# A third early expert slot, the last weight sums outside the fixed order, and a later fetch of the late slots' tables

## The chip, the cores and the metric

The kernel runs on one core of one Trainium2 chip. The metric is the device time of one execution in microseconds (us). Before the change the median of 3 runs is 879.53 us (878.68 to 882.45).

## The reference: what is computed

Two stages follow each other. The first is a hashed attention: 4 batches, 8 heads, 768 positions, 64 values a head. Each query and each key gets a bucket from the signs of six projections, a query looks only at keys of its own bucket, and the softmax of the masked scores weighs the values.

```python
mask = q_bucket[:, :, :, None] == k_bucket[:, :, None, :]
scores = scale * np.matmul(q, k.transpose(0, 1, 3, 2))
scores = np.where(mask, scores, -1000000000.0)
...
x = np.ascontiguousarray(attn_out.transpose(0, 2, 1, 3)).reshape(B * S, H * D)
```

The second is a mixture of experts over the 3072 tokens x of 512 values: each token goes to the one expert of eight with the largest logit and is weighted by its softmax.

```python
logits = x @ w_gate + modality_bias[modality_id]
e_idx = np.argmax(logits, axis=1)
...
    h = np.maximum(x[mask] @ w1[e], 0.0)
    out[mask] = gate_w[mask, None] * (h @ w2[e])
```

With the inputs as drawn two experts get nearly all tokens: after the first three batches (2304 tokens) experts 1 and 3 have 1124 and 1099 of them, which is four full blocks of 256 tokens each, eight in all.

## The kernel before, in words

**Attention stage.** Heads are taken in pairs, 16 pairs, four to a batch. The PE's order in this stage is written out by hand (`tc.manual_schedule` over PE in `attention`, with the string `PLAN`): scores, exponentials, row maxima and the weighing of the values of neighbouring pairs are interleaved. For each pair `score` lets POOL (sometimes DVE) add up the exponentials over the key tiles (line 326), and `sums` (line 359) multiplies the result with ones on PE, so that the weights' sums stand ready for the division. In the order of PE `sums(i - 1)` stands inside of the next pair (letter Q); that of the last pair, `sums(NPR - 1)` at line 514, stands at the end of the fixed order.

**After a batch.** `finish(b)` (lines 366 to 412) projects the batch's result on the gate weights, turns it and divides it, and its last part, `route` (lines 589 to 636), finds each token's expert and place and writes the tokens' records into the table `tab` in DRAM with six indirect DMAs of POOL (line 631, the scatter). `finish_x` (lines 415 to 427) turns the attention result itself, divides it and writes it to `x_d` in DRAM, six tiles a batch, through two buffers `xs` (DVE line 424, DMA line 426; for the last batch on ACT's queue). For the first three batches these steps lie inside of the fixed order of a later batch.

**Expert stage.** The work is cut into slots. A big slot has 256 tokens of one expert, a small one 128. A slot runs through eight pieces of weights: pieces 0 to 3 are quarters of `w1` (`gemm1`, lines 793 to 795), pieces 4 to 7 quarters of `w2` (`gemm2`, lines 835 to 837). `Runner.slot(k)` (line 882 and on) runs them. `ahead` keeps SP loading weights (lines 748 and 750, 512 KB a piece) up to seven pieces ahead in four buffers, and ACT and DVE (for odd pieces of the first eight POOL) splitting them in a high and a low part (lines 756 and 758). `fetch` reads a slot's expert and place from the slot table, reads its token records with a DMA of SP (line 766, `tb`) and gathers the tokens' rows from `x_d` with one indirect DMA of POOL for each 128 tokens (line 770, `xg`). `prepare` also turns the rows on PE (line 781, eight transposes for a big slot) and splits them (ACT line 782, DVE line 783). In slot k the next slot is prepared at piece 4; the two slots after it are fetched at piece `CFG["fj"]`, which is 0, when k > 0.

**Early and late slots.** The first `EARLY` = 2 slots ("e") hold only full blocks of tokens of the first three batches, so that their tables are known before the last batch is through. `early_slots` finds them. Then `body` fetches and prepares slot e0, fetches e1, and because EARLY is 2 runs all of `finish(3)`, then `late_slots` (some forty small DVE operations, lines 642 to 713), and only then slot 0, interleaved with `finish_x(3)`. The late slots are 12 - EARLY = 10 big ones ("b") and 2 small ones ("s"). Their records come from `tab`, so that SP's read of it waits for the scatter, and their rows from `x_d`, so that POOL's gather waits for all writes of it. The gather of an early slot reads only the rows of the first three batches; its read of `tab` waits for those scatters that stand ahead of it in the program. More than the sure number of slots run in conditional blocks behind the last slot; with these inputs none does, 12 big and 2 small slots cover all tokens.

**Order.** Outside of the fixed order an instruction's place on its engine is found when the program is built, by its place in the program and by when its inputs are expected. Each engine then works through its list in order; whatever waits holds all behind it.

Of the kernel before, what the change touches and what calls it, by code (L numbers as in the profile page):

```python
# [18 lines left out]
B, H, S, D = 4, 8, 768, 64  # L19
# [3 lines left out]
REST = S - MAIN  # L23
NP = B * H // 2
BIG = 2.0 ** 100
CFG = dict(spd=(15,), fxs=3, wy=(0.3, 0.71), hpf=0, he=0, hn=0, hm=0, avp=(1, 2, 3, 4, 5, 6), avs=(2,), early=2, w3=(0, 0.9), x3=(0, 1), nmd=1, man=(), man0=2, hpo=0, hpe=0, p0=(0, 1), p1=(0, 0.25), p2=(0, 0.4), p3=(0.4, 0.9), s0=4, rc='DDDD', rq=(1, 2), tq=(3, 3, 1, 1, 0, 0), wh=(0.5, 0.78), ws=(0.78, 1.05), n2=2, psx=2, psm=2, pss=2, npb=4, ut=8, qk=3, v=2, wm=(0, 0.9), wf=(0.04, 1.02), wx=(0.3, 0.71), sub="DPPD", fx='D', fx3='R', raw=4, wp=7, LS=4, LL=7, pn=8, rv=(0,), rs='DDPP', r1=(0, 0.5), r2=(0, 1), avg=1, fub=2, fd=2, pm=(), fj=0, fxe=1.0)
P = 128

LAG = 2
# [45 lines left out]
def attention(ctx, actx, tc, a, x_d, l_d, route=None, setup=None):  # L75
    nc = tc.nc
    q, k, v, proj = a["q"], a["k"], a["v"], a["proj"]
    NPR = a.get("npair", NP)
    fconst = ctx.enter_context(tc.tile_pool(name="fconst", bufs=1))
    spool = ctx.enter_context(tc.tile_pool(name="spool", bufs=2))  # L80
    upool = ctx.enter_context(tc.tile_pool(name="upool", bufs=CFG["ut"]))
    bp = ctx.enter_context(tc.tile_pool(name="bp", bufs=1))
    ps_x = ctx.enter_context(tc.tile_pool(name="ps_x", bufs=CFG["psx"], space=PSUM))
    nat = actx.enter_context(tc.tile_pool(name="nat", bufs=CFG["n2"]))
    ld = actx.enter_context(tc.tile_pool(name="ld", bufs=CFG["qk"]))
    gens = []
    for g in range(3):
        opp = actx.enter_context(tc.tile_pool(name=f"opp{g}", bufs=1))
        gens.append({n: [opp.tile([P, S], F32R, name=f"{n}_{h}g{g}") for h in range(2)] for n in ("m1", "s1", "m2", "s2")})
    ldv = actx.enter_context(tc.tile_pool(name="ldv", bufs=CFG["v"]))  # L90
    sm = actx.enter_context(tc.tile_pool(name="sm", bufs=4))
    const = actx.enter_context(tc.tile_pool(name="const", bufs=1))
    ps_m = actx.enter_context(tc.tile_pool(name="ps_m", bufs=CFG["psm"], space=PSUM))
    ps_s = actx.enter_context(tc.tile_pool(name="ps_s", bufs=CFG["pss"], space=PSUM))
# [5 lines left out]
    def load(i, heads=(0, 1)):  # L100
        b, c = i // 4, i % 4
        t = st.setdefault(i, {"qk": []})
        for h in heads:
            qk = ld.tile([P, 2, NT, D], F32, name="qk")
            t["qk"].append(qk)
            for x, src in enumerate((q, k)):
                nc.sync.dma_start(out=qk[:, x], in_=src[b, 2 * c + h].rearrange("(p t) d -> p t d", t=NT))

    def load_v(i):
        b, c = i // 4, i % 4  # L110
        t = st[i]
        t["v"] = ldv.tile([P, 2, NT, D], F32, name="vt")
        nc.sync.dma_start(out=t["v"], in_=v[b, 2 * c:2 * c + 2].rearrange("h (p t) d -> p h t d", t=NT))
# [238 lines left out]
    def sums(i):  # L352

        b, c = i // 4, i % 4
        if c == 0:
            gsum[b] = bp.tile([P, HALF], F32, name="gs")
        g = ps_x.tile([P, MAIN], F32, name="psx")
        for j in range(4):
            nc.tensor.matmul(g[32 * j:32 * j + 32, 0:HALF], ones[:, c], st[i]["sp"][:, j // 2, (j % 2) * HALF:(j % 2 + 1) * HALF],
                             start=True, stop=True, tile_position=(0, 32 * j))  # L360
        if c == 0:
            nc.vector.tensor_copy(out=gsum[b], in_=g[:, 0:HALF])
        else:
            nc.vector.tensor_tensor(out=gsum[b], in0=gsum[b], in1=g[:, 0:HALF], op=ALU.add)
# [80 lines left out]
    with tc.manual_schedule(engines={mybir.EngineType.PE}):  # L445
        load(1)
        load_v(0)
        load(2)
        first()
        wg = sm.tile([P, 4, 8], F32, name="wg", bufs=1)  # L450
        nc.sync.dma_start(out=wg, in_=a["moe_w_gate"].rearrange("(c p) e -> p c e", p=P))
        gst = fconst.tile([P, 4, 32], F32, name="gst")
        nc.gpsimd.memset(gst, 0.0)
        nc.gpsimd.tensor_copy(out=gst[0:64, :, 0:8], in_=wg[0:64])
        nc.gpsimd.tensor_copy(out=gst[64:128, :, 16:24], in_=wg[64:128])
        ones = fconst.tile([P, 4, 32], F32, name="ones")
        nc.gpsimd.memset(ones, 0.0)
        for c in range(4):
            nc.gpsimd.memset(ones[:, c, c:c + 1], 1.0)
        if setup is not None:  # L460
            setup()
        avs = weigh()
        fins = xs = ts = iter(())
        for i in range(NPR):
            late = []
            ss = score(i)
            ms = maxp(i + 1, late) if i + 1 < NPR else iter(())
            last, ts = ts, chain(turn(i + 2), signs(i + 2), patterns(i + 2)) if i + 2 < NPR else iter(())
            ws = split(i + 3) if i + 3 < NPR else iter(())
            if i % 4 == 0 and i > 0:  # L470
                fins = finish(i // 4 - 1)
            for kt in range(NT):
                for c in PLAN[kt]:
                    if c == "S":
                        next(ss)
                    elif c == "M":
                        next(ms, None)
                    elif c == "T":
                        next(ts, None)
                    elif c == "P":  # L480
                        next(last, None)
                    elif c == "W":
                        next(ws, None)
                    elif c == "A":
                        if i > 0 or kt >= LAG:
                            next(avs)
                    elif c == "B":
                        if late:
                            late.pop(0)()
                    elif c == "v":  # L490
                        vadds(i)
                    elif c == "V":
                        vsums(i)
                    elif c == "Q":
                        if i > 0:
                            sums(i - 1)
                    elif c == "L":
                        if i + 3 < NPR:
                            load(i + 3)
                    elif c == "l":  # L500
                        if i + 1 < NPR:
                            load_v(i + 1)
                    elif c == "F" and i % 4 == 0 or c == "f" and i % 4 == 1:
                        next(fins, None)
                    elif c == "e" and i % 4 >= 2 or c == "E" and i == NPR - 2:
                        next(fins, None)
                    elif c == "x" and i % 4 == 2 or c == "y" and i % 4 == 3:
                        if c == "x" and kt == 0 and i > 4:
                            xs = finish_x(i // 4 - 1, 0, NT)
                        next(xs, None)  # L510
                        next(xs, None)
        for _ in avs:
            pass
        sums(NPR - 1)
    return finish, finish_x, ps_x, ident


# [6 lines left out]
EARLY = CFG["early"]  # L524
# [194 lines left out]
def experts(ctx, tc, a, x_d, tab, out, ps_x, ident):  # L719
# [3 lines left out]
    raw = ctx.enter_context(tc.tile_pool(name="raw", bufs=CFG["raw"]))  # L723
# [122 lines left out]
    class Runner:  # L846
# [35 lines left out]
        def slot(self, k):  # L882
            s = self.order[k]
            nxt = self.order[k + 1] if k + 1 < len(self.order) else None
            self.prepare(s)
            hh, hl, h = [], [], None
            for j in range(8):
                self.ahead()
                if j == CFG["fj"] and k > 0:
                    for s2 in self.order[k + 1:k + 1 + CFG["fd"]]:  # L890
                        self.fetch(s2)
                if j == 4:
                    yps = [ps_y.tile([P, DM], F32, name="yps") for _ in range(nt(s))]
                    if nxt:
                        self.prepare(nxt)
                hi, lo = self.ws.pop(self.n)
                if j >= 4:
                    gemm2(j, hi, lo, hh, hl, yps)
                elif nt(s) == 2:
                    gemm1(hi, lo, *self.xs[s], hh, hl)  # L900
                else:
                    last, h = h, gemm1_small(hi, lo, *self.xs[s])
                    if last is not None:
                        turn_small(last, hh, hl)
                if j == 4 and h is not None:
                    turn_small(h, hh, hl)
                self.n += 1
                yield
            store(self.got[s][0], yps)
# [73 lines left out]
```

## Time and profile before

| what | us |
|---|---|
| median of 3 runs | 879.53 |
| lowest, highest | 878.68, 882.45 |
| profiled execution, its own time | 876.6 |
| its span, first to last instruction | 874.7 |
| PE busy | 815.4 (93%) |
| DVE busy | 584.8 (67%) |
| ACT busy | 506.2 (58%) |
| POOL busy | 457.1 (52%) |

The profile was taken from one execution. The span is what the rows' times count from; 876.6 - 874.7 = 1.9 us lie outside of it. PE is the tensor engine, DVE the vector engine, ACT the scalar engine, POOL GpSimd, SP the engine that issues most DMAs. A busy PE is not a PE at its peak: matmuls overlap, and the time from one start to the next (0.12 us for a 256-column one in the expert stage) is shorter than what a row gives as one's duration.

### The profile page before, as it was taken

The page shows a single profiled execution, that of the slowest core. Times are in us where ns is not written, and L with a number is a line of the kernel's source. Part 1 is how long each engine was busy: PE and PEld are TensorE (multiplying, and loading weights), DVE is VectorE, ACT ScalarE, POOL GpSimd, SP SyncE. Part 2 cuts the span into 40 slices and gives each one's busy share as a digit, 9 for nine tenths or more (in the row PEclk, how much of TensorE's full clock was granted, in tenths as well). Part 3 has the DMA queues.
Part 4 walks back from the last instruction along what each step waited for, and adds up shares of the span by engine and source line. Part 5 has one row for each costly group of instructions (what it writes and reads, how often), then busy time and mean ns, then how long its engine had stood idle before and what let it go on. Part 6 is the DMA issues. An engine that isn't in the chain of part 4 may idle for free.

```text
span 874.7 us, 14543 instructions
## 1 busy us (share of the span) xinstructions
PE 815.4 (93%) x5154; PEld 579.8 (66%) x5154; DVE 584.8 (67%) x1029; ACT 506.2 (58%) x953; POOL 457.1 (52%) x347
## 2 busy tenths in 40 slices
PE   5899999998999998999998898879999999999993
PEld 3555655654665554665554555779999999998993
DVE  7776676678677678667776876955555555667550
ACT  5666766665666565566664364444555555557551
POOL 5387678757688757687756687322222221123010
PEclk9899999999999999999999999999999999999997
DMA  6423212221332321340210163796777776677750
GB/s 178 115 60 91 64 41 77 74 54 55 98 85 72 91 60 32 97 118 22 55 46 9 31 229 120 166 266 196 230 231 218 222 227 215 209 240 267 229 155 22
DMA packets 76753, 110.87 MB, mean 127 GB/s; under 512 B 10495, under 2 KB 52095, under 8 KB 76672
## 3 DMA queue, kind: packets, MB, share of 16 engines
q1 hardware_dynamic: 70880, 95.14, 37.6%
q0 software_dynamic: 4928, 13.14, 4.0%
q10 hardware_dynamic: 864, 1.57, 0.9%
q8 instruction: 43, 0.70, 0.4%
q14 instruction: 38, 0.31, 0.1%
HBM read 84.83 MB, written 13.33 MB: 112 GB/s over the span
## 4 chain that ended last, share of the span: by engine, by line
PE 77%; DVE 10%; ACT 4%; DMA 3%; issue 3%; POOL 2%; SPq 0%; POOLq 0%; ACTq 0%; DVEq 0%
PE psu L341 14%; PE pss L305 8%; PE pss L306 6%; PE psm L239 5%; PE yps L835 5%; PE yps L837 5%; PE yps L836 5%; PE hps L795 4%; PE hps L794 4%; PE hps L793 4%; PE psx L207 3%; PE psx L180 3%; PE psm L245 3%; PE psx L222 2%; DVE mx L241 1%
## 5 line engine op out<-in xcount | busy, mean ns | idle before, releaser
L326 POOL TENSOR_TENSOR sp<-sp,pb 128x768 f32<-128x768 f32 x124 | 225.3, 1841 | 42.0 <-ACT pb L323 40.6
L758 DVE TENSOR_TENSOR w<-raw,w 128x1024 fp32r<-128x1024 f32 x108 | 134.9, 1250 | 94.4 <-ACT w L756 93.3
L756 ACT CAST w<-raw 128x1024 fp32r<-128x1024 f32 x112 | 117.2, 1047 | 63.2 <-PE yps L837 55.9
L341 PE MATMUL psu<-pb,vt 128*64 128x512 f32 (+1 forms) x768 | 147.0, 505 | 0.0
L241 DVE TENSOR_REDUCE mx<-psm 128x1 f32<-128x512 f32 x192 | 127.6, 685 | 23.1 <-PE psm L239 22.4
L318 ACT ACTIVATE pb<-pss 128x512 f32<-128x512 f32 x192 | 114.9, 599 | 42.3 <-PE pss L306 22.8
L323 ACT ACTIVATE pb<-pss 128x512 f32<-128x512 f32 x96 | 57.5, 599 | 125.7 <-PE pss L306 122.8
L793 PE MATMUL hps<-xh,w 128*128 128x256 f32 x384 | 108.9, 284 | 2.4 <-DVE hl L800 2.4
L794 PE MATMUL hps<-xl,w 128*128 128x256 f32 x384 | 108.9, 284 | 0.0
L795 PE MATMUL hps<-xh,w 128*128 128x256 f32 x384 | 108.5, 283 | 0.0
L341 PEld LDWEIGHTS psu<-pb,vt 128*64 128x64 f32 x768 | 47.2, 137 | 88.4 <-issue 88.2
L770 POOL DMA_INDIRECT xg<-x_d,tb x26 | 30.8, 1184 | 125.9 <-DMA tb<-tab 87.7
L843 POOL DMA_INDIRECT out<-y,tb x26 | 34.0, 1309 | 118.0 <-ACT y L842 61.3
L835 PE MATMUL yps<-w,hl 128*128 128x512 f32 x208 | 83.6, 402 | 1.9 <-DVE hl L823 1.9
L837 PE MATMUL yps<-w,hh 128*128 128x512 f32 x208 | 81.8, 393 | 0.0
L836 PE MATMUL yps<-w,hh 128*128 128x512 f32 x208 | 81.7, 393 | 0.0
L247 DVE TENSOR_REDUCE mx<-psm 128x2 f32<-128x512 f32 x96 | 66.1, 689 | 22.7 <-PE psm L245 21.5
L305 PE MATMUL pss<-m_0g,s_0g 128*128 128x512 f32 x192 | 78.2, 407 | 0.0
L793 PEld LDWEIGHTS hps<-xh,w 128*128 128x128 f32 x384 | 73.4, 192 | 3.7 <-DVE hl L800 3.0
L166 POOL TENSOR_TENSOR n<-qk,n 128x384 fp32r<-128x384 f32 x36 | 39.7, 1109 | 67.3 <-ACT n L162 60.0
L794 PEld LDWEIGHTS hps<-xl,w 128*128 128x128 f32 x384 | 73.6, 192 | 1.7 <-issue 1.2
L795 PEld LDWEIGHTS hps<-xh,w 128*128 128x128 f32 x384 | 73.5, 192 | 0.0
(214 smaller groups left out, 1763.0 us busy)
## 6 DMA issues: line engine op xcount, KB each, us to landing
raw<-moe_w SPq DMA_DIRECT2D x112, 512.0 KB
qk<-q SPq DMA_DIRECT2D x32, 192.0 KB
qk<-k SPq DMA_DIRECT2D x32, 192.0 KB
vt<-v SPq DMA_DIRECT2D x16, 384.0 KB
x_d<-xs SPq DMA_DIRECT2D x18, 256.0 KB
m_1g<-m_1g SPq DMA_DIRECT2D x16, 192.0 KB
s_1g<-s_1g SPq DMA_DIRECT2D x16, 192.0 KB
m_0g<-m_0g SPq DMA_DIRECT2D x15, 192.0 KB
```

Of the source, the lines that this page charges most:

```text
L241: nc.vector.tensor_reduce(out=mx[:, qt + j, hi, 0:1], in_=mp, axis=AX.X, op=ALU.max)
L305: nc.tensor.matmul(out, t["s1"][h][:, ks], t["m1"][h][:, cs], start=True, stop=False)
L326: (nc.vector if h and i in CFG["spd"] else nc.gpsimd).tensor_tensor(out=t["sp"][:, h], in0=(t["pb"][0] if kt == 1 else t["sp"])[:, h], in1 ...
L341: nc.tensor.matmul(t["u"][part][64 * h:64 * h + 64, 0:w], t["v"][:, h, kt], t["pb"][kt][:, h, COLS[part]], start=False, stop=(kt == NT - 1 ...
L756: nc.scalar.copy(out=hi, in_=r)
L758: (nc.gpsimd if pool else nc.vector).tensor_tensor(out=lo, in0=r, in1=hi.bitcast(F32), op=ALU.subtract)
L793: nc.tensor.matmul(hps, lo[:, c, fs], xh[:, c], start=(c == 0), stop=False)
L794: nc.tensor.matmul(hps, hi[:, c, fs], xl[:, c], start=False, stop=False)
L795: nc.tensor.matmul(hps, hi[:, c, fs], xh[:, c], start=False, stop=(c == 3))
L835: nc.tensor.matmul(yps[g], hl[fc][:, gs], hi[:, fb], start=(fc == 0), stop=False)
L836: nc.tensor.matmul(yps[g], hh[fc][:, gs], lo[:, fb], start=False, stop=False)
L837: nc.tensor.matmul(yps[g], hh[fc][:, gs], hi[:, fb], start=False, stop=(fc == 7))
```

## The change

Three edits. `early=3` makes three early slots and, by `SURE_BIG = 12 - EARLY`, nine late big ones; it also takes the other branch in `body`: slot 0 is interleaved with `finish(3)` (its 14 nominal steps spread over the first 0.9 of the slot), slot 1 with `finish_x(3)`, and `late_slots` follows behind slot 1. `sums(NPR - 1)` moves out of the block of the fixed order. The late slots' fetch moves from piece 0 to piece 4 in the slot EARLY - 1, which is now the third one; in all others it stays at piece 0.

```diff
--- before.py
+++ after.py
@@ -23,7 +23,7 @@
 REST = S - MAIN
 NP = B * H // 2
 BIG = 2.0 ** 100
-CFG = dict(spd=(15,), fxs=3, wy=(0.3, 0.71), hpf=0, he=0, hn=0, hm=0, avp=(1, 2, 3, 4, 5, 6), avs=(2,), early=2, w3=(0, 0.9), x3=(0, 1), nmd=1, man=(), man0=2, hpo=0, hpe=0, p0=(0, 1), p1=(0, 0.25), p2=(0, 0.4), p3=(0.4, 0.9), s0=4, rc='DDDD', rq=(1, 2), tq=(3, 3, 1, 1, 0, 0), wh=(0.5, 0.78), ws=(0.78, 1.05), n2=2, psx=2, psm=2, pss=2, npb=4, ut=8, qk=3, v=2, wm=(0, 0.9), wf=(0.04, 1.02), wx=(0.3, 0.71), sub="DPPD", fx='D', fx3='R', raw=4, wp=7, LS=4, LL=7, pn=8, rv=(0,), rs='DDPP', r1=(0, 0.5), r2=(0, 1), avg=1, fub=2, fd=2, pm=(), fj=0, fxe=1.0)
+CFG = dict(spd=(15,), fxs=3, wy=(0.3, 0.71), hpf=0, he=0, hn=0, hm=0, avp=(1, 2, 3, 4, 5, 6), avs=(2,), early=3, w3=(0, 0.9), x3=(0, 1), nmd=1, man=(), man0=2, hpo=0, hpe=0, p0=(0, 1), p1=(0, 0.25), p2=(0, 0.4), p3=(0.4, 0.9), s0=4, rc='DDDD', rq=(1, 2), tq=(3, 3, 1, 1, 0, 0), wh=(0.5, 0.78), ws=(0.78, 1.05), n2=2, psx=2, psm=2, pss=2, npb=4, ut=8, qk=3, v=2, wm=(0, 0.9), wf=(0.04, 1.02), wx=(0.3, 0.71), sub="DPPD", fx='D', fx3='R', raw=4, wp=7, LS=4, LL=7, pn=8, rv=(0,), rs='DDPP', r1=(0, 0.5), r2=(0, 1), avg=1, fub=2, fd=2, pm=(), fj=0, fxe=1.0)
 P = 128
 
 LAG = 2
@@ -511,7 +511,7 @@
                         next(xs, None)
         for _ in avs:
             pass
-        sums(NPR - 1)
+    sums(NPR - 1)
     return finish, finish_x, ps_x, ident
 
 
@@ -886,7 +886,7 @@
             hh, hl, h = [], [], None
             for j in range(8):
                 self.ahead()
-                if j == CFG["fj"] and k > 0:
+                if j == (4 if k == EARLY - 1 else 0) and k > 0:
                     for s2 in self.order[k + 1:k + 1 + CFG["fd"]]:
                         self.fetch(s2)
                 if j == 4:
```

The branch in `body` that is now taken, word for word (line numbers of the text before):

```python
        if EARLY > 2:
            drive([(r.slot(0), 8, 0, 1), (finish(B - 1), 14, *CFG["w3"])])
            drive([(r.slot(1), 8, 0, 1), (finish_x(B - 1, 0, NT), 12, *CFG["x3"])])
            k = 2
```

The fetch of the third early slot, e2, stands in slot 1 at piece 0, behind `finish(3)` in the program, so that its read of `tab` comes behind the last scatter. The fetch of the first late slots, b0 and b1, stands in slot 2 at piece 4.

## Rows read from the trace of the kernel before

**Rows 1.** Busy time by stretch: us, then PE, PEld, DVE, ACT, POOL; clock, DMA share, GB/s

```profile
533.30:570.60 37.30, 32.55 (x229) 26.55 (x230) 31.47 (x96) 16.64 (x26) 16.26 (x12) 1.00 0.65 156
570.60:601.30 30.70, 25.82 (x153) 22.75 (x152) 16.31 (x21) 13.33 (x21) 7.10 (x7) 0.94 0.75 240
601.30:624.60 23.30, 23.30 (x153) 21.40 (x152) 14.04 (x18) 13.16 (x21) 5.55 (x5) 1.00 0.73 226
```

**Rows 2.** PE in order of time: start, us; idle before and releaser in brackets

```profile
587.98 1.24 PE L781 MATMUL psx<-ident,xg 128*128 128x128 f32 x7 [2.61 <-DMA xg<-x_d,tb]
...
612.82 1.03 PE L781 MATMUL psx<-ident,xg 128*128 128x128 f32 x8
```

**Rows 3.** PE groups, 533.3 to 601.3 us: busy, mean ns, idle before

```profile
L422 PE MATMUL psx<-ident,ut 128*128 128x128 f32 x24 | 3.7, 276 | 0.0
L374 PE MATMUL psx<-ut,gst 128*32 128x512 f32 (+1 forms) x16 | 1.7, 498 | 0.1
L383 PE MATMUL psx<-ident,gsb 128*128 128x128 f32 x6 | 1.0, 281 | 0.7 <-DVE gsb L375 0.7
```

**Rows 4.** PE in order of time, where the attention stage ends

```profile
530.49 2.80 PE L341 MATMUL psu<-pb,vt 128*64 128x512 f32 x16
534.62 0.85 PE L359 MATMUL psx<-sp,ones 128*32 128x384 f32 x8 [1.33 <-POOL sp L326]
```

**Rows 5.** Waits of PE, 533 to 602 us: total, times, longest

```profile
PE psx L781 <- DMA xg<-x_d,tb: 3.1, 2, 2.6
PE hps L793 <- DVE hl L800: 2.4, 3, 1.4
PE psx L781 <- DVE over L712: 1.3, 1, 1.3
PE psx L359 <- POOL sp L326: 1.3, 1, 1.3
...
PE psx L609 <- DVE oh L604: 0.6, 1, 0.6
```

**Rows 6.** Busy time by stretch, columns as in the first group

```profile
588.60:591.90 3.30, 3.30 (x11) 2.72 (x10) 2.42 (x3) 1.14 (x3) 0.00 (x0) 0.50 0.81 300
...
540.00:560.00 20.00, 18.09 (x145) 16.06 (x138) 19.70 (x58) 7.64 (x15) 8.88 (x7) 1.00 0.66 214
```

**Rows 7.** SP's DMA issues in order of time

```profile
501.42 0.36 SPq L766 DMA_DIRECT2D tb<-tab  x1
...
571.88 1.20 SPq L766 DMA_DIRECT2D tb<-tab  x2
...
606.98 0.37 SPq L748 DMA_DIRECT2D raw<-moe_w  x1
...
619.93 0.35 SPq L766 DMA_DIRECT2D tb<-tab  x1
```

**Rows 8.** POOL in order of time: indirect DMAs that it issues

```profile
496.01 0.96 POOL L631 DMA_INDIRECT tab<-rec,posi  x1 [0.30 <-issue]
...
562.53 0.96 POOL L631 DMA_INDIRECT tab<-rec,posi  x1 [0.30 <-issue]
...
585.52 0.97 POOL L770 DMA_INDIRECT xg<-x_d,tb  x1 [0.30 <-issue]
...
623.43 1.82 POOL L770 DMA_INDIRECT xg<-x_d,tb  x1 [11.70 <-DMA tb<-tab]
625.56 0.97 POOL L770 DMA_INDIRECT xg<-x_d,tb  x1 [0.30 <-issue]
```

**Rows 9.** DVE in order of time

```profile
545.48 2.07 DVE L402 TENSOR_SCALAR f<-rin 128x48 f32<-128x48 f32 x1
...
561.20 0.25 DVE L677 TENSOR_REDUCE selr<-selx 128x13 f32<-128x104 f32 x1
...
572.74 1.29 DVE L424 TENSOR_TENSOR xs<-psx,rin 128x512 f32<-128x512 f32 x2 [4.05 <-DMA x_d<-xs]
...
623.17 1.22 DVE L758 TENSOR_TENSOR w<-raw,w 128x1024 fp32r<-128x1024 f32 x1 [1.49 <-ACT w L756]
```

## The prediction

> **What bounds the kernel now.** Read first the busy time by stretch, then PE's order and its waits where the stages meet, then the queues of SP, POOL and DVE there.
>
> In a settled slot PE is the bound: slot 2 takes 23.3 us and PE is busy for all of it, with DVE at 14.04 and the clock full [rows 1]. The work of the slots is the same after the change (12 big and 2 small), so nothing can be won there. The place to look is between the two stages, from 533.3 us, where the last weighing of values on PE ends (530.49 + 2.80) [rows 4], to 601.30, where slot 2 begins. These 68.0 us are slot 0 (533.3 to 570.6) and slot 1 (570.6 to 601.3), and PE is not full in either [rows 1].
>
> How much is lost there? Slot 0 takes 37.3 us. Its own work is 23.3, the transposes of e0 ahead of it 1.0 [rows 2] and the weights' sums 0.85 [rows 4]. The steps of the last batch that PE does in it (projection, turning, finish_x) show as 3.7 + 1.7 + 1.0 us and some small ones, about 7.7 [rows 3]; but these are busy times with overlapping tails, and start to start is about two thirds of them, my estimate 5.0 (2.3 of it finish_x). 37.3 - 23.3 - 1.0 - 0.85 - 5.0 = **7.1 us lost in slot 0**. Slot 1 takes 30.7 for work of 23.3: **7.4 lost**. Together 14.5, and that is the most the change can find.
>
> The waits say where [rows 5]. In slot 0: 1.3 for POOL's last addition ahead of the sums, 0.7 [rows 3] and 0.6 for finish's DVE steps, 1.3 for the last DVE step of late_slots (an x-preparation buffer is free only behind it), 0.6 of the 2.4 for `hl`; the remaining 2.6 are gaps too small for a row while the first weights are split, DVE being busy 19.70 of 20 us between 540 and 560 [rows 6]. In slot 1: 1.8 us for `hl`, behind a DVE that stood 4.05 us at `xs` until a write of x_d had landed [rows 9]; 3.1 us for the gather of b0's rows; and behind that wait 3.3 us at clock 0.50, the lower of the two levels (1.2 and 2.4 GHz), which costs 1.7 us [rows 6]. That is 6.6 of 7.4.
>
> So the end is set by a chain of latencies: attention's end, finish(3), scatter, the read of `tab`, writes of x_d, gather, transposes at slot 1's piece 4.
>
> **The change part by part.**
>
> *Sums outside the fixed order.* The eight matmuls (0.85 us) stay; what goes is that e0's transposes stand behind their wait. e0's gather was issued before, so PE can start slot 0 at 533.3. Gain 1.3 [rows 4]; below, nothing, if the place stays the same.
>
> *late_slots behind slot 1.* The 1.3 us wait for its last step leaves slot 0. The DVE work itself, some forty operations like the one at 561.20 (0.25 us, about half that from start to start, so some 5 us) [rows 9], now falls into slot 1 or 2, where DVE has 23.3 - 14.04 = 9.3 us to spare a slot [rows 1]; cost nothing there, and if that cover were gone up to 5.
>
> *finish(3) beside slot 0.* The same instructions, none added. With lower rank its DVE steps no longer push back the splits of slot 0, but its own chain gets no shorter. Of the 2.6 us of small gaps and the 1.9 of waits for DVE I keep 3.3 between them, since DVE's work in slot 0 is nearly the same (bounds 1.7 and 5.8, which is 7.1 less the sums' wait). Slot 0 then is 23.3 + 1.0 + 0.85 + 2.7 + 3.3 = 31.2 us and ends at 564.5.
>
> *finish_x(3) beside slot 1.* Its 2.3 us of PE, six DVE multiplications and six writes on ACT's queue move from slot 0 to slot 1. A multiplication waits for the write two before it; with one every 4 us the 4.05 us stall [rows 9] should shrink. Behind it on DVE stand `hl` and `xl`, for which PE waits. I take 1.0 for what PE loses by it, between 0 and the 1.8 of now.
>
> *The third early slot.* This is the added wait. e2's read of `tab` stands on SP behind the last scatter, exactly as b0's did, but its gather needs no row of x_d from the last batch. Before, SP read at 571.88, as soon as the scatter had landed, 9.4 us after its last issue at 562.53 [rows 7, 8]; SP's weight loads stood behind that, but they run a slot ahead of use. From there: read to first gather 3.5 us (619.93 to 623.43), two gathers 2.1 apart (623.43 to 625.56), last gather to its landing 2.5 (585.52 to 587.98) [rows 2, 7, 8]. If finish(3) keeps its pace, e2's rows are there at 571.88 + 3.5 + 2.1 + 2.5 = 580.0. PE reaches piece 4 of slot 1 11.5 us after the slot's start (601.30 to 612.82) [rows 1, 2] and half of finish_x, 1.2: 564.5 + 11.5 + 1.2 = 577.2. That is a wait of 2.8 us, and 1.7 of low clock behind it, if the transposes stand first in piece 4, as they did before. But the scatter of the batch before was read 5.4 us after its last issue (496.01 to 501.42) [rows 7, 8], when no write of x_d and few loads lay beside it; now the x_d writes come later, so the landing may be up to 4.0 us sooner and the wait gone. Between 0 and 4.5 I take 2.0. With 1.0 for `xs` and 0.5 of small gaps slot 1 loses 3.5.
>
> *The later fetch.* b0's rows are needed for slot 3 now, whose preparation stands at piece 4 of slot 2, and the fetch stands at the same piece. x_d and `tab` have landed long before, so nothing of the last batch is waited for. SP reads `tab` behind the weight load that it has just issued; in slot 2 of before the fourth load went out at 606.98, 5.8 us ahead of piece 4's transposes at 612.82 [rows 2, 7]. The chain from read to landing is 3.5 + 2.1 + 2.5 = 8.1, so the rows come 2.3 us into piece 4, plus 1.7 of low clock if PE stands. If the transposes' place in PE's order allows for that, nothing is lost; if the read only goes out when piece 4 begins, 8.1 + 1.7 = 9.8 are. The nearest row is the steady lead, so I take 1.7, less than the full 4.0 because four pieces of gemm2 can be placed ahead.
>
> *SP, POOL and ACT queues.* One `tab` read and two gathers become early ones, one pair fewer is late; counts are the same. POOL's queue holds only output stores behind the gathers, which nobody waits for in these slots.
>
> **Sum.** Lost after: 3.3 + 3.5 + 1.7 = 8.5 us against 14.5, a gain of **6.0**. The profiled execution goes from 876.6 to 870.6. The median of the runs is 2.9 above the profiled one; on that level 879.5 - 6.0 = **873.5 us**. A measurement of this kernel can tell about 0.5%, 4.4 us, from no change.
>
> **The rivals.**
>
> *All waits covered.* The transposes of e2 and b0 land in PE's order where their data has come, and finish is hidden behind slot 0: 1.7 + 1.0 + 0.3 lost, 11.5 us gained, **868.0**. For it: PE's order already mixes finish's matmuls among gemm1's, and 11 us of gemm2 stand free in each slot. Against it: b0's transposes of before stood first in piece 4 and waited [rows 2].
>
> *Given back.* The stall of slot 1 stays and a second one comes in slot 2: 3.3 in slot 0, 2.8 + 1.7 + 1.5 in slot 1, 2.3 + 1.7 in slot 2, 13.3 in all; gain 1.2, **878.3**. For it: the chain from attention's end to e2's rows is as long as the way to piece 4, within 3 us.
>
> *Slower: POOL's issues held by DVE.* e2's rows hang on eight POOL issues in a row, six scatters and two gathers. An issue takes 0.96 us free, but the one at 623.43 took 1.82 [rows 8]: DVE was at a weight split from 623.17 to 624.39 [rows 9]. The other way round, DVE's `f` took 2.07 us for 48 elements beside a weight split of POOL [rows 9]. If each of the eight takes 0.9 more, e2's rows come 7.2 later: slot 1 loses 2.8 + 7.2 + 1.7 + 1.5 = 13.2, slot 2 2.3 + 1.8 + 1.7 = 5.8, slot 0 3.3; 22.3 in all, 7.8 more than now, **887.3**. It decides from a loss of 18.9 on. Against it: the last scatter took 0.96 with DVE over nine tenths busy [rows 6, 8]. The Trainium skill, page "SBUF — State Buffer", section "Who interferes with whom", says that a DVE instruction with two SBUF inputs and a GpSimd instruction that reads SBUF lock each other out of a shared port for a whole instruction; it speaks against putting the scatter beside the splits, the 2.07 and 1.82 agree with it, and the 0.96 does not.
>
> *Not what it says.* If fewer than three full blocks existed after three batches, the third slot would run empty and one late slot would move into the conditional part, at least 23.3 us more. Eight exist with these inputs.
>
> **How the numbers follow.** The forecast 0.46, all covered 0.15, given back 0.25, slower 0.12, not what it says 0.02. Faster by over 0.5% (under 875.1) are the covered case and nearly all of the forecast's: 0.58. Within 0.5%: the given-back case and the forecast's edge, 0.30. Slower: 0.12. The range goes from 867.5, the covered case, to 882.0, the given-back case with the upper bound of the later fetch half taken; it leaves out the slow tail and the fastest runs.
>
> **What would show it.** In the profile after: no wait of PE for POOL's `sp` at the sums, and transposes of e0 before them; slot 0 ending near 564 and slot 2 beginning near 594 in place of 601.3; SP's read for e2 near 570 behind the scatter; a PE wait for `xg` of 0 to 4 us at piece 4 of slot 1, and one of 0 to 4 in slot 2; slots from the fourth on at 23.3. The prediction is wrong if a wait over 5 us stands at one of the two gathers, if slot 0 still takes over 34 us, or if the clock falls in slots 0 to 2 for longer than 3.4 us.

## The result and the profile after

The changed kernel is slower: **887.12 us** median of 16 runs (881.35 to 890.68) against 877.57 of the kernel before (872.90 to 882.45), ratio 1.0098 with a 95% interval of 1.0078 to 1.0117. By this ratio, which is the measure from here on, 8.6 us are lost; the two medians differ by 9.6. The prediction, 873.5 us and at most 882.0, was wrong in sign and range. The profiled execution takes 886.66 us (span 884.9), 10.1 more than that of before.

Where is it lost? The busy time by stretch, cut as in [rows 1]: slots 0, 1, 2 and 3, then the bad place in slot 1, then two places of the attention stage (columns: us, PE, PEld, DVE, ACT, POOL; clock, DMA share, GB/s).

```profile
536.91:567.34 30.43, 29.18 (x211) 24.37 (x210) 26.22 (x64) 17.41 (x28) 13.11 (x9) 1.00 0.54 173
567.34:606.01 38.67, 29.65 (x176) 26.40 (x174) 20.78 (x54) 13.10 (x20) 9.31 (x8) 0.82 0.56 191
606.01:634.57 28.56, 25.20 (x154) 22.49 (x152) 14.17 (x18) 13.35 (x21) 8.01 (x7) 0.94 0.65 204
634.57:657.88 23.31, 23.31 (x153) 21.40 (x152) 14.04 (x18) 13.16 (x21) 5.47 (x5) 1.00 0.74 226
581.50:595.10 13.60, 7.60 (x29) 6.44 (x30) 6.80 (x10) 5.23 (x9) 2.51 (x3) 0.50 0.98 347
...
204.00:210.00 6.00, 5.14 (x22) 1.76 (x23) 3.91 (x10) 1.51 (x3) 2.88 (x3) 0.72 0.26 67
333.00:339.00 6.00, 3.98 (x13) 1.30 (x11) 5.26 (x10) 2.59 (x6) 4.31 (x3) 0.73 0.15 33
```

Slot 0 is 6.9 us shorter than before, as forecast. Slot 1 is 8.0 longer, slot 2 5.3 longer, and from slot 3 on all is as it was. From attention's end to slot 3 (the **hand-over** from here on) it is 97.65 us against 91.31: **6.3 us more**. Of the other 3.9 us between the two spans, 3.6 lie ahead of 536.91: about 1.6 at each of two falls of the clock, in the last two rows, where it is 1.00 before, and 0.3 at the start. PE's order up to there is the same in both kernels, and the falls show in some of the later profiles and not in others, whatever the edit (below), so they are not counted to the change.

PE in order of time shows the places, to be held beside [rows 2, 4].

```profile
537.98 0.85 PE L359 MATMUL psx<-sp,ones 128*32 128x384 f32 x8 [1.06 <-POOL sp L326]
...
586.35 0.58 PE L793 MATMUL hps<-xh,w 128*128 128x256 f32 x1 [7.86 <-DVE hl L800]
...
590.51 0.45 PE L781 MATMUL psx<-ident,xg 128*128 128x128 f32 x1 [0.38 <-DMA xg<-x_d,tb]
591.73 0.90 PE L781 MATMUL psx<-ident,xg 128*128 128x128 f32 x3 [0.77 <-DMA xg<-x_d,tb]
...
617.99 0.39 PE L837 MATMUL yps<-w,hh 128*128 128x512 f32 x1
621.74 0.41 PE L781 MATMUL psx<-ident,xg 128*128 128x128 f32 x2 [3.36 <-DMA xg<-x_d,tb]
```

In slot 1 PE hardly waits for e2's rows: 0.38 and 0.77 us. It stands 7.86 us in the middle of gemm1, for `hl` of DVE, and then works at clock 0.50. What held `hl`? ACT in order of time:

```profile
573.36 0.39 ACT L799 ACTIVATE hh<-hps 128x256 fp32r<-128x256 f32 x1 [1.05 <-PE hps L795]
583.66 1.04 ACT L756 CAST w<-raw 128x1024 fp32r<-128x1024 f32 x1 [9.91 <-DMA raw<-moe_w]
...
584.61 0.65 ACT L799 ACTIVATE hh<-hps 128x256 fp32r<-128x256 f32 x2
```

ACT stood 9.91 us at the split of a weight piece (the first of slot 2, which PE needs at 606); the rectified tiles `hh`, from which `hl` is made, were queued behind it. DVE's part of the same split stood 9.16 us for ACT's, with `hl` behind it in DVE's queue:

```profile
584.74 1.23 DVE L758 TENSOR_TENSOR w<-raw,w 128x1024 fp32r<-128x1024 f32 x1 [9.16 <-ACT w L756]
```

And why was the piece late? SP's issues in order of time, and SP's waits (total, times, longest):

```profile
552.27 10.04 SPq L750 DMA_DIRECT2D raw<-moe_w  x4
579.34 0.35 SPq L766 DMA_DIRECT2D tb<-tab  x1
580.24 2.24 SPq L748 DMA_DIRECT2D raw<-moe_w  x4
...
612.86 1.26 SPq L766 DMA_DIRECT2D tb<-tab  x2
```

```profile
SPq L766 <- DMA tab<-rec,posi: 16.5, 1, 16.5
```

SP stood 16.5 us at e2's read of `tab`, which waits for the scatter, and issued no load meanwhile. Then four went out in 2.24 us. The chain of waits goes the same way and on to e2's rows:

```profile
572.13 7.19 DMA tab<-rec,posi
...
579.34 1.66 DMA tb<-tab
...
582.35 0.99 POOL xg L770
...
583.64 8.04 DMA xg<-x_d,tb
```

### The profile page after: what moved, and what is told of

It reads as the page before. It is cut to its first block, busy times and chain, and to the rows that moved or that the text cites. A ratio compares the mean times of both kernels' runs of the same rounds, so it can differ in the third digit from the quotient of the medians.

```text
span 884.9 us, 14543 instructions
## 1 busy us (share of the span) xinstructions
PE 822.2 (93%) x5154; PEld 582.5 (66%) x5154; DVE 583.2 (66%) x1029; ACT 507.1 (57%) x953; POOL 459.9 (52%) x347
## 5 line engine op out<-in xcount | busy, mean ns | idle before, releaser
L341 PE MATMUL psu<-pb,vt 128*64 128x512 f32 (+1 forms) x768 | 149.8, 513 | 0.0
L770 POOL DMA_INDIRECT xg<-x_d,tb x26 | 32.5, 1250 | 114.3 <-DMA tb<-tab 107.2
L837 PE MATMUL yps<-w,hh 128*128 128x512 f32 x208 | 82.1, 394 | 0.0
```

The lines of the kernel that those rows point to most:

```text
L341: nc.tensor.matmul(t["u"][part][64 * h:64 * h + 64, 0:w], t["v"][:, h, kt], t["pb"][kt][:, h, COLS[part]], start=False, stop=(kt == NT - 1 ...
L837: nc.tensor.matmul(yps[g], hh[fc][:, gs], hi[:, fb], start=False, stop=(fc == 7))
```

## The experiments

**Theory Q (queue):** the loss in slot 1 is SP's queue, held at e2's read, passed through ACT's queue to PE. **Rival L (late rows):** e2's rows come too late for slot 1 anyway, so that without the queue PE only stands at the transposes instead. For slot 2 the theory is that the loss comes from the place of the fetch, piece 4. Each ratio is to runs of the kernel before on the same chip.

### One place at a time

The third early slot stays in all kernels of this part but sums_alone.

**e2_ahead**, to the kernel after: e2 is fetched ahead of `finish(3)`, where its read waits for no scatter of the last batch.

```diff
         r.fetch(("e", 1))
+        r.fetch(("e", 2))
```

> The changed kernel with e2's table and rows fetched right behind e1's, ahead of finish(3) in the program, so that its read does not wait for the last scatter. Theory Q (SP's queue: the read of e2's table stood 16.5 us behind the scatter, weight piece 16 behind it, ACT's split of it 9.9 us, the rectified tiles behind that, PE 7.9 us): the 7.9 us gap of PE in slot 1 goes, and with it the wait for e2's rows and most of the 13.7 us at clock 0.50; slot 1 falls from 38.7 to 27 or 28 us, the total by 9 to 11 us, to about 877, below the kernel before or level with it. Rival D (DVE and ACT are simply overfull in slots 0 and 1, the queue only shows it): slot 1 stays over 33 us and the total falls by less than 4.

Measured: 882.69 us, 1.0044 (1.0015 to 1.0072), so about 4.7 us of after's 8.6 are won, less than the full stall with its clock and half of what I expected. SP's, ACT's and the 7.86 us wait are gone, but slot 1 still takes 33.3 us, not 27 or 28, and other waits show (by total, times, longest; the last is slot 2's):

```profile
DVE xs L424 <- DMA x_d<-xs: 6.1, 2, 3.5
...
ACT hh L799 <- DVE xs L424: 5.8, 2, 4.2
PE psx L781 <- DVE xs L424: 5.3, 2, 3.8
PE psx L781 <- DMA xg<-x_d,tb: 4.0, 1, 4.0
```

Now DVE stands at `xs`, two buffers wide, for a write of x_d, and PE behind it. Q holds for what it names; a second bound lay under it. The rival D of the expectation (DVE and ACT overfull) is not decided by this run: slot 1 stays over 33 us as it says, but more than 4 us are won. both_xs6 below decides it: there slot 1 falls to 26.4 us with as much work on both engines.

**fetch_back**, to the kernel after: the late slots' fetch at piece 0 again.

```diff
-                if j == (4 if k == EARLY - 1 else 0) and k > 0:
+                if j == 0 and k > 0:
```

> The changed kernel with the third edit undone: the late slots' tables are fetched at piece 0 of slot 2 again. Theory Q: slot 1 stays as it is (38.7 us, gap of 7.9); slot 2 loses its 3.4 us wait for b0's rows and the 3.4 us at clock 0.50 behind it, and falls from 28.6 to about 24; the total falls by 4 to 5 us. Rival: at piece 0 the read waits for something else (the writes of x_d), and slot 2 stays at 27 or more.

Measured: 880.24 us, 1.0031 (1.0014 to 1.0049); 5.9 us are won, a little over the 4 to 5 expected. Slot 2 by stretch:

```profile
608.42:631.71 23.29, 23.29 (x153) 21.40 (x152) 14.04 (x18) 13.15 (x21) 7.65 (x7) 1.00 0.77 253
```

PE is full and the clock too. The later fetch is a pure loss here.

**sums_back** (after with the sums in the fixed order) and **sums_alone** (before with them outside):

```diff
-    sums(NPR - 1)
+        sums(NPR - 1)
```

> The changed kernel with the second edit undone: the last weight sums stand in the fixed order again. PE's order at that place came out the same in both profiles (wait for POOL's addition, sums, then e0's transposes), so no change: within 1 us of the changed kernel. Rival: the edit shifts other engines' order in the last pair and costs up to 4 us, which would show as an attention stage that ends near 533 and not 537.

> The kernel before with the second edit alone. As its order on PE keeps the sums ahead of e0's transposes, the time stays within 1 us of the kernel before. Rival: 1 to 4 us faster by the wait of 1.3 us that goes, or slower by 2 to 4 us if this edit is what made the attention stage end later.

Measured: 886.59 us, 1.0097 (1.0074 to 1.0120), and 877.41 us, 0.9998 (0.9976 to 1.0020). The edit does nothing. PE in order of time in sums_back, beside after's 537.98:

```profile
538.52 0.85 PE L359 MATMUL psx<-sp,ones 128*32 128x384 f32 x8 [1.05 <-POOL sp L326]
539.31 0.66 PE L781 MATMUL psx<-ident,xg 128*128 128x128 f32 x4
```

In both the sums keep their wait and their place ahead of e0's transposes. Leaving the fixed order did not move them.

**both_fetches**: e2_ahead and fetch_back together.

> The changed kernel with e2 fetched ahead of finish(3) and the late slots' fetch back at piece 0: the third early slot without either of the two late fetches. If the two costs add (5 us and 6 us against the changed kernel's 887): 876 to 877, level with the kernel before, with waits of 5 us left in slot 1 for the finish_x multiplications behind their writes of x_d. Rival: they do not add (the fetch at piece 0 of slot 2 now comes while x_d is still being written and its gather waits), 879 to 881.

Measured: 876.38 us, 0.9974 (0.9951 to 0.9997). Against after's 1.0098 that is 10.9 us, and the two alone are 4.7 + 5.9 = 10.6: **the two costs add within their intervals, and together they are more than the whole loss.** With both undone the third early slot is a gain, barely. Slot 1 by stretch:

```profile
570.23:605.66 35.43, 28.88 (x176) 25.56 (x174) 21.00 (x54) 12.99 (x20) 7.57 (x6) 0.86 0.76 182
```

It is only 3.2 us shorter than in after. PE stands 6.5 us there for `xs`: a write of x_d takes up to 11.8 us to land, against 8.0 before, and a buffer is free only then.

### Queue or late rows

**e2_read_pool**, to the kernel after: only e2's read of `tab` goes out on POOL's queue, so that SP does not stand at the scatter.

```diff
+        own = s == ("e", 2)
...
-        nc.sync.dma_start(out=tb[:, 0:n], ...)
+        (nc.gpsimd if own else nc.sync).dma_start(out=tb[:, 0:n], ...)
```

> The changed kernel with e2's read of its table issued from POOL's queue in place of SP's; the read waits for the scatter as before, but no weight load stands behind it. Theory Q: SP's 16.5 us wait, ACT's 9.9 us wait for weight piece 16 and PE's 7.9 us gap before the last piece of gemm1 in slot 1 go; what is left is the lateness of the rows themselves, 4 to 8 us of waiting at e2's transposes and a clock fall behind it, so the total falls by 2 to 5 us from 887. Rival L (late rows alone made the loss, the queue did not matter): PE's wait in slot 1 moves from the gap to the transposes in full, over 10 us there, and the total stays within 2 us of 887.

Measured: 888.71 us, 1.0135 (1.0100 to 1.0170). SP's wait, ACT's and the gap are gone, and nothing is won: PE's and POOL's order of time say why.

```profile
593.60 0.45 PE L782 MATMUL psx<-ident,xg 128*128 128x128 f32 x1 [11.58 <-DMA xg<-x_d,tb]
```

```profile
573.61 0.95 POOL L631 DMA_INDIRECT tab<-rec,posi  x1 [0.30 <-issue]
...
584.38 0.59 POOL L767 DMA_DIRECT2D tb<-tab  x1 [7.99 <-DMA tab<-rec,posi]
```

PE now stands 11.58 us at e2's transposes. By the total L is right, and Q's waits were real as well: both bounds are there, one behind the other. And the scatter itself is later: its read goes out 584.38 - 573.61 = 10.8 us after the last issue, against 579.34 - 572.13 = 7.2 in after, where SP was silent.

**e2_j7** (after, with e2's rows turned at piece 7 of slot 1) and **e2_read_pool_j7** (the same on e2_read_pool):

```diff
-                    if nxt:
-                        self.prepare(nxt)
+                if j == (7 if k == 1 else 4) and nxt:
+                    self.prepare(nxt)
```

> The changed kernel with e2's rows turned at piece 7 of slot 1 in place of piece 4, so that PE has some 8 us of gemm2 ahead of them. Theory Q (the way through SP's queue, the late weights and ACT is enough by itself): the gap of 7.9 us ahead of the last piece of gemm1 and the fall of the clock stay, and only the 1 to 3 us of waiting at the transposes go; the total falls by 1 to 3 us. Theory L (PE just meets the late rows): the gap shrinks, and the total falls by 6 us or more.

> The kernel e2_read_pool (e2's read on POOL's queue, so that no weights wait) with e2's rows turned at piece 7 of slot 1. Now both ways from the late scatter to PE are widened. Theory of two ways (the queue and the rows each cost about the same, and either is enough): the 11.6 us wait at the transposes falls to 2 to 4 us, slot 1 from 41 to 30 or 32, the total by 8 to 11 us, to 878 to 881. Rival: the rows come later still, or the end of the slot waits for them in the next one, and less than 4 us are won.

Measured: 884.57 us, 1.0098 (1.0060 to 1.0136), and 884.20 us, 1.0100 (1.0067 to 1.0133). In the first a gap of 6.76 us at `hl` and the low clock stay: the stall is not the transposes'. By ratio nothing is won, though slot 1 of its profile is 4.4 us shorter (34.3). In the second PE still waits 4.96 and 2.31 us for e2's rows, with three pieces of room; I had expected 8 to 11 us to be won and got about 3. A latency that hangs on the last scatter does not fit into slot 1 at any of these places.

**finish_first**, to the kernel after: `finish(3)` whole ahead of slot 0, as before.

```diff
-            drive([(r.slot(0), 8, 0, 1), (finish(B - 1), 14, *CFG["w3"])])
+            for _ in finish(B - 1):
+                pass
+            drive([(r.slot(0), 8, 0, 1)])
```

> The changed kernel with finish(3) run whole ahead of slot 0 in the program, as before the change, and slot 0 alone behind it; e2's read still stands behind the scatter. Theory P (e2's rows came late because finish(3), with lower rank, reached its scatter 4.1 us later after the attention's end than before): the scatter begins 22 to 23 us after the attention's end in place of 26.8, e2's rows come 4 us or more sooner, slot 1 falls by 4 to 6 us, slot 0 grows by 2 to 4; the total falls by 0 to 3 us. Rival: the pace of finish is no part of it; the scatter lands no sooner, and the total is level or higher by what slot 0 grows.

Measured: 884.14 us, 1.0083 (1.0053 to 1.0113). POOL's first and last scatter and SP's read of `tab`, in order of time:

```profile
561.01 1.72 POOL L631 DMA_INDIRECT tab<-rec,posi  x1 [8.57 <-DVE posi L628]
...
568.10 1.22 POOL L631 DMA_INDIRECT tab<-rec,posi  x1 [0.30 <-issue]
```

```profile
578.88 0.35 SPq L766 DMA_DIRECT2D tb<-tab  x1
```

The scatter begins 22.8 us after attention's end (538.26) in place of 26.8 (563.73 - 536.91), so finish's lower rank did cost its chain 4 us. The read of `tab` gains only 1.8 of them (578.88 - 538.26 = 40.6 in place of 42.4), since it goes out 10.8 us after the last issue. Slot 1 is 6.3 us shorter and slot 0 2.9 longer; the total lies in the interval of after, so that the trade is near even.

### What lies behind, and a faster version

**both_xs6**: both_fetches, with six buffers for the last batch's `xs` in a pool of their own, and **before_xs6**, the same buffers in the kernel before.

```diff
+        xsp = ctx.enter_context(tc.tile_pool(name="xsp", bufs=1))
...
-            xs = bp.tile([P, 512], F32, name="xs", bufs=2)
+            xs = (pool or bp).tile([P, 512], F32, name="xs", bufs=6 if pool else 2)
```

> The kernel both_fetches with six buffers xs in place of two for the last batch's finish_x (in the space that the attention stage leaves). Theory X (in e2_ahead DVE waited 6.1 us and ACT 5.8 us at finish_x for writes of x_d, and PE 5.3 us for the buffers behind them): these waits go, slot 1 falls to 26 to 27 us, the total to 869 to 873, below both kernels. Rival: the writes are not what holds (the scatter's traffic slows the loads as well), slot 1 stays over 30 and the total at 875 or more.

> The kernel before with six buffers xs for the last batch's finish_x alone. Theory X: DVE's 4.05 us wait and ACT's 6.2 us go, the last two writes of x_d go out some 8 us sooner, the gather of b0 lands ahead of its transposes; 3 to 6 us faster than before, 871 to 874. Rival: the six writes then fall together with the scatter and land no sooner; within 1.5 us of before.

Measured: 872.46 us, 0.9931 (0.9904 to 0.9958), and 879.99 us, 1.0020 (0.9996 to 1.0043). With both fetches right, the buffers bring slot 1 to 26.4 us, but slot 0 grows from 31.8 to 33.5: the pool stands ahead of those of the weights, and ACT waits 7.9 us in all for loads (1.8 in both_xs6_behind). So the pool was put behind them: **both_xs6_behind** and **before_xs6_behind**, where only that line moves.

> The kernel both_xs6 with the six buffers taken behind the expert stage's own in memory and not ahead of them. In both_xs6 ACT waited 7.9 us for weights in slot 0 and slot 0 took 33.5 us in place of 31.8. If the place of the buffers held the first weights back: slot 0 falls by 1 to 2 us and the total to 870 to 872. If the order of the memory plays no part: within 1 us of both_xs6.

> The kernel before with six buffers xs, now behind the expert stage's own in memory. before_xs6 gained nothing, but its buffers lay ahead of the weights' and may have held the first weights back. If that hid a gain: 2 to 5 us faster than before, with slot 0 at 36 us or less. If the two early slots gain nothing from the buffers, since b0's rows also hang on the scatter: within 2 us of before, slot 1 still 29 us or more.

Measured: **867.86 us, 0.9913 (0.9883 to 0.9943)**, the fastest of all, and 877.63 us, 1.0005 (0.9980 to 1.0029). Slots 0 to 2 of the fastest by stretch, and slot 0 of both_xs6:

```profile
535.37:567.52 32.15, 29.58 (x209) 24.43 (x210) 27.81 (x64) 17.39 (x28) 15.28 (x10) 1.00 0.60 192
567.52:594.15 26.63, 26.20 (x175) 23.53 (x174) 21.03 (x54) 12.88 (x20) 7.56 (x6) 1.00 0.85 225
594.15:617.45 23.30, 23.30 (x153) 21.41 (x152) 13.88 (x18) 13.05 (x21) 7.75 (x7) 1.00 0.82 270
```

```profile
539.01:572.47 33.46, 29.77 (x211) 24.43 (x210) 30.54 (x66) 18.75 (x29) 20.20 (x11) 1.00 0.75 232
```

The clock is full throughout and the hand-over 82.1 us against 91.3 before. The pool's place gives 1.0 us in the hand-over; the two ratios' intervals overlap. With two early slots the same buffers bring nothing by the times. The profile of before_xs6_behind does show a shorter hand-over (87.5 us, with slot 0 at 35.9 and slot 1 at 28.3, as the expectation of a gain had it); that its times do not show this stays open. Its slot 1 still waits for rows that hang on the last scatter; PE in order of time:

```profile
579.71 0.39 PE L793 MATMUL hps<-xh,w 128*128 128x256 f32 x1 [1.71 <-DVE hl L800]
...
590.09 0.98 PE L781 MATMUL psx<-ident,xg 128*128 128x128 f32 x7 [2.21 <-DMA xg<-x_d,tb]
```

**best_finish_first**: the fastest, with `finish(3)` whole ahead of slot 0 (the diff of finish_first).

> The kernel both_xs6_behind (three early slots, none of them behind the scatter, six buffers) with finish(3) run whole ahead of slot 0. Nothing early hangs on the scatter here any more, so finish gains nothing by being early. Theory P (its first rank costs slot 0 the 3 us that finish_first showed there): slot 0 rises from 32 to 34 or 35, the total by 2 to 3 us to about 870. Rival: rank does not matter, within 1 us of 868.

Measured: 873.52 us, 0.9950 (0.9928 to 0.9973), about 3 us more by ratio, with overlapping intervals and the same hand-over in its profile (82.2 us; slot 0 takes 32.5, not the 34 or 35 expected). The profiled execution, 869.5 us, is one of the faster ones, so it does not show where the 3 us lie. Where nothing hangs on the scatter, finish's low rank costs nothing that these runs show; whether it gains 3 us stays open. The buffers in the kernel after, with its two late fetches, were not tried.

The clock falls near 206 and 336 us are absent in the profiles of before, sums_alone, e2_read_pool_j7 and both_xs6_behind, and present in those of before_xs6 and before_xs6_behind, whose attention stage is that of before. The change is not what brings them. That leaves 6.3 us of the medians' 8.6 (by ratio) located in the profile; the rest stays open.

## Why the prediction was wrong, step by step

- **Slot 0**: the size is right, 31.2 forecast and 30.4 measured, but partly by luck. The sums' wait of 1.06 us that the forecast left out is still in it, and of the 3.3 us kept for small gaps and waits for DVE about 1.5 are there.
- **Sums**: 1.3 us forecast, nothing came. The lower bound ("nothing, if the place stays the same") was the truth; what I took rested on the program's order and not on PE's, which did not change.
- **late_slots** behind slot 1 and **finish(3)** beside slot 0: the 1.3 us wait left slot 0 as forecast. DVE's work did not move behind slot 1, though: it runs from 562.69 to 574.9, across the end of slot 0. And "if finish(3) keeps its pace" failed: 4.1 us later at the scatter, shown by finish_first.
- **The third early slot** is the step that failed: 3.5 us of loss forecast for slot 1, 38.67 - 23.3 - 2.3 = 13.1 measured. That is 9.6 of the 12.4 us between the forecast hand-over (91.3 - 6.0 = 85.3) and the measured 97.7. First, its sentence on SP's weight loads, "they run a slot ahead of use", is true for PE and not for ACT, whose split of a piece stands in ACT's queue 22 us ahead of PE's use (583.66 against 606), among the `hh` that PE needs at once. The wait of one queue became that of a second and a third: 16.5 us on SP, 9.91 on ACT, 9.16 on DVE, 7.86 on PE (e2_ahead takes them away). Of the 13.1, 7.9 are this gap, 1.2 the waits for rows, and 7.60 us of PE's work at clock 0.50 account, by halving, for 3.8. Second, its chain from attention's end to e2's rows was too short: 46.7 us in the sum, 54.8 measured, and its only bound from lateness reached to 4.5. Half of these 8.1 us is a misreading of rows of before. The sum took the last gather's landing as 2.5 us, from the gather at 585.52 to PE's transposes at 587.98 [rows 2, 8]. The gather at 585.52 is b1's; PE waited for b0's second one, issued at 581.35, as the chain of waits of before has it:

```profile
581.35 6.59 DMA xg<-x_d,tb
```

That is 6.6 us, and the shortest landing of any gather that the traces show is 3.3 (e2_ahead). With 6.6 the same sum has e2's rows at 584.1, 6.9 us behind PE, and its upper bound is 8.6 with the clock, not 4.5. The rest: finish's pace 4.1, slower scatter issues 1.9, and 1.4 more for the last gather, 8.04 us beside the four loads that had piled up; the landing of the scatter gave back 2.1, the read and the gathers' spacing 1.3.
- **The later fetch**: mechanism right, size wrong. 1.7 us taken, 28.56 - 23.3 = 5.3 measured. Read to rows took 8.9 us (612.86 to 621.74; 8.1 in the sum). PE reached the transposes 5.5 us after the read (618.38) in place of 5.8, although only three gemm2 matmuls were put ahead of them, so nothing of the cover that I took for half the price was there. Wait 3.36, clock 1.7: the row's own price, 4.0 with its bounds, was the better choice. That the sum's 8.1 is near is luck: its 2.5 was too short here too, but the wait ended with the first gather (616.58, landed 5.02 us later) and not with the second.
- **`xs`**: I took 1.0 us. In after it stays hidden behind the other stall; in e2_ahead it shows with 5.3 us of PE's wait. Between both_fetches and both_xs6 slot 1 falls from 35.4 to 26.4 us, so some 9 hang on it: with both fetches in time the gain is 2.3 us by ratio and not 6.0, and this term is what is left. Its upper end, "the 1.8 of now", was an end only for the order of before.
- **Rival "slower"**: its 887.3 us is near the result, for other reasons. Of its mechanism 1.9 us are there (below), not 7.2.
- **Forecast gain**: it exists. With both fetches ahead of their need and six buffers, three early slots take 867.86 us, by 1.0005 against 0.9913 some 8 us less than two with the same buffers. It is also the 868.0 of the rival in which all waits are covered, reached with three edits more.

## What to carry to other kernels

A DMA that waits for something late holds its whole queue: list what is queued behind it, for every engine that takes that data, and look at the first use in that engine's own queue, not at the last user's. Fetch ahead of a slow producer whatever does not need it, and bound a moved step's lateness as well as its earliness. Before a wait goes into a sum, follow it to the very row that ended it: the nearest issue ahead of it can belong to another transfer. When one wait goes, ask which buffer or table is next: here the two late fetches and the two buffers all had to go before the change paid clearly.

## What was unexpected of the hardware

**POOL's issues and DVE's weight splits.** Scatter issues by POOL and weight splits by DVE in the kernel after, in order of time:

```profile
563.73 1.75 POOL L631 DMA_INDIRECT tab<-rec,posi  x1 [12.58 <-DVE posi L628]
...
570.06 1.77 POOL L631 DMA_INDIRECT tab<-rec,posi  x1 [0.30 <-issue]
572.13 0.96 POOL L631 DMA_INDIRECT tab<-rec,posi  x1 [0.31 <-issue]
```

```profile
563.38 1.23 DVE L758 TENSOR_TENSOR w<-raw,w 128x1024 fp32r<-128x1024 f32 x1
...
569.77 1.22 DVE L758 TENSOR_TENSOR w<-raw,w 128x1024 fp32r<-128x1024 f32 x1
...
572.83 1.21 DVE L758 TENSOR_TENSOR w<-raw,w 128x1024 fp32r<-128x1024 f32 x1
```

An issue that begins during a split ends 0.87 and 0.84 us after the split's end (565.48 against 564.61, 571.83 against 570.99), about as if it started there; one that begins before the split (572.13) takes its free 0.96 us. From 540 us on, 25 issues of this profile begin during a split and end 0.82 to 1.00 us after its end; 16 begin before one and take 0.95 to 1.03. Who begins first decides. It agrees with the Trainium skill, page "SBUF — State Buffer", section "Who interferes with whom", by which a DVE instruction with two SBUF inputs contends with a GpSimd instruction that reads SBUF, and the order of issue decides who waits. The prediction held the 0.96 us of the scatter at 562.53 [rows 8] against that rule, but no split ran beside it: DVE's splits nearest to it run from 557.65 to 558.87 and from 564.86 on.

**The scatter's landing** differs much, from the last issue to the read: 7.2 us with SP silent, 9.4 before and 5.4 for the batch ahead [rows 7, 8], 10.8 with weight loads running (e2_read_pool), and again 10.8 in finish_first, where SP stands at the read too, but has issued loads until 566.03, 2 us ahead of the last scatter. Loads that are still moving would fit all five; that they are the cause was not tried alone.

**The price of a gap.** With 7.86 us without work PE's clock stood at 0.50, the lower of its two levels, for the 13.6 us of the row above (581.5 to 595.1), from within the gap to 9 us after it. At half the clock 7.60 us of work cost PE some 3.8 (an estimate, by halving), half as much again as the gap itself.
